# The opening of an eight-batch attention, gated MLP and expert-attention kernel: one written list of single steps for all engines

## The chip, the cores and the metric

The kernel runs on one core of a Trainium2 chip. The metric is the device time of one execution in microseconds. TensorE (PE in the profile) does the matrix products and transposes, VectorE (DVE) and ScalarE (ACT) work on their results, GpSimd (POOL) does small side work, and SyncE (SP) issues the transfers (DMAs); it has one queue, in which a transfer that waits holds up all behind it.

## What is computed

For each of eight batches: a packed attention (32 query rows `p` over the 576 rows of `k` and `v`, then `q` over the packed rows), an MLP whose second half is mixed over the tokens by `w_sg`, and a causal attention in each of four experts, of which two count per token.

```python
def sm_attn(qq, kk, vv): ...                       # softmax(qq kk^T / 8) vv
p_packed = sm_attn(p, k, v); x = sm_attn(q, p_packed, p_packed)   # [8, 576, 512] after the heads are joined
h = gelu(x @ w_in); u, v = h[..., :512], h[..., 512:]
v_n = (v - mean(v)) / sqrt(var(v) + 1e-6) * g_ln
gated = u * (einsum('ts,bsd->btd', w_sg, v_n) + b_sg)
x = x + gated @ w_out
# experts e: q, k, v = x @ wq[e], x @ wk[e], x @ wv[e]; causal softmax; ye = a @ v @ wo[e]; top 2 of 4 by x @ w_gate
```

## The kernel before

**Weights.** `moe_w_in` (two halves `f`: 0 makes u, 1 makes v; four tiles `j` each) and `moe_w_out` (four tiles `c`) come as 64-bit floats and are turned to 32 bits on VectorE and ScalarE: six VectorE instructions of 128x512 per tile (L150, L151, L160 to L163) and one on ScalarE (L155). `w_out` is then multiplied into the expert weights: `prep_w_out` transposes a tile, `fold` makes 4 products into PSUM (512, 256 and 4 columns), `fold_out` splits the result into a high and a low part. Products of split operands run in three passes (`PASSES`). `w_sg` is transposed by `prep_w_sg`, five tiles, and split too.

**Batch 0.** Steps named by letters in the table `STEP`: K (transpose k on TensorE), s (scores of p), n, a (transpose them), Q (transpose q), p (packed product), P (transpose it), m (scores of q, L448), x, r (their softmax on VectorE), h (split them). Then `w'` (`wp_mm`, L625: packed rows times `w_in`), the v products (`v_tiles`, L676), the token mixing (`vs_mm`, L744), the u products (`u_tile`, L726) and the gate. In `startup` these are written in one order, stage after stage.

**Batches 1 to 7.** k and q are not transposed on TensorE but in transfers: each of 16 heads (8 of k, 8 of q) is turned by a DMA transpose into a tile `kx` or `qx` (two buffers), which a second transfer writes to DRAM (`turned_k`, `turned_q`); `planes` loads them back (`kp`, `qp`), and GpSimd joins the two halves of each word (L416, 8 instructions for k and 8 for q). The turns are queued in the list `TURN`, one head per entry, each entry first writing out the head before:

```python
TURN.append([lambda a=last: a and keep(*a), lambda a=(name, src, h): turn(*a)])
```

`tick()` takes one entry. `back(0)`, after the gate, runs the last stage of batch 0 (`bdw`, the products `qk`, `vlog`) mixed with the packed attention of batch 1.

**What sets the order.** In `startup` only TensorE follows the written order (`manual_schedule(engines={ET.PE})`); the framework's scheduler orders the other engines and SP's queue. From `back(0)` on, TensorE and SP both follow the written order. PSUM has four working tiles (`pd`), and the SBUF tiles come from rings: the three buffers of tag "a" hold the raw `w_in` tiles, the two of "W" the expert weights of the folds and later `w_qk` and `w_vg`, the ten of "B" the softmax, the split v and `kp` and `qp`.

Of the kernel before, what the change touches and what calls it, by code (L numbers as in the profile page):

```python
# [7 lines left out]
F32 = mybir.dt.float32  # L8
# [18 lines left out]
def packed_attention_mlp_moe_kernel(  # L27
# [80 lines left out]
    nc.sync.dma_start(g_bc, dap(moe_g_ln, 0, [[0, P], [1, DM]]))  # L108
# [39 lines left out]
    def from_f64_top(raw, dst):  # L148
        hw, top = words(raw)[:, :, 1], dst.bitcast(I32)
        nc.vector.tensor_scalar(top, hw, 3, 0x3FFFFFF8, op0=OP.logical_shift_left, op1=OP.bitwise_and)  # L150
        nc.vector.scalar_tensor_tensor(top, hw, -0x40000000, top, op0=OP.bitwise_and, op1=OP.bitwise_or)  # L151

    def from_f64_abs(raw):
        hw = words(raw)[:, :, 1].bitcast(F32)
        nc.scalar.activation(hw, hw, AF.Abs)  # L155

    def from_f64_low(raw, dst, pw):
        lw, hw, top = words(raw)[:, :, 0], words(raw)[:, :, 1], dst.bitcast(I32)
        f = pw.bitcast(F32)
        nc.vector.tensor_scalar(pw, top, -0x800000, None, op0=OP.bitwise_and)  # L160
        nc.vector.scalar_tensor_tensor(f, lw.bitcast(U32), 2.0 ** -52, f, op0=OP.mult, op1=OP.mult)
        nc.vector.tensor_tensor(f, f, dst, op=OP.add)
        nc.vector.scalar_tensor_tensor(dst, hw.bitcast(F32), LEAST_F64, f, op0=OP.is_ge, op1=OP.mult)  # L163
# [26 lines left out]
    w_in = {}  # L190

    def w_in_steps(f):
        def top(j):
            w_in[f, j] = slot("D", w=512, name="w_in")
            from_f64_top(raw_in[f, j], w_in[f, j])

        def low(j):
            from_f64_low(raw_in[f, j], w_in[f, j], nat_slot(I32, "pw"))
            nc.sync.dma_start(kept[f"in{f}"][:, j, :], w_in[f, j])

        return top, lambda j: from_f64_abs(raw_in[f, j]), low
# [3 lines left out]
    def load_w_all():  # L205

        t = slot("W", name="fqk").rearrange("p (i e r d) -> p i e r d", i=2, e=E, r=4)
        g = slot("W", w=1040, name="fvg")
        v = g[:, :1024].rearrange("p (e r d) -> p e r d", e=E, r=4)
        for o, w in ((t[:, 0], moe2_wq), (t[:, 1], moe2_wk), (v, moe2_wv)):  # L210
            nc.sync.dma_start(o.rearrange("p e r d -> p e (r d)"), dap(w, 0, [[4 * D, P], [DM * D, E], [1, 4 * D]]))
        nc.sync.dma_start(g[:, 1024:], dap(moe2_w_gate, 0, [[4 * E, P], [1, 4 * E]]))
        for r in range(4):
            folded[r] = (t[:, :, :, r, :].rearrange("p i e d -> p (i e) d"), v[:, :, r, :],
                         g[:, 1024 + 4 * r:1028 + 4 * r])
# [13 lines left out]
    def prep_w_sg(c):  # L229
        n = TOK[c]  # L230
        st = wst[c]
        pw = pd("wsgT")
        pt, pl = pw[:, 0, :], pw[:, 1, :]
        for a in range(4):
            nc.tensor.transpose(pt[:, a * P:a * P + n], st[:n, a * P:(a + 1) * P], ident[:n, :n])
        nc.tensor.transpose(pl[:64, 0:n], st[:n, 512:576], ident[:n, :n])
        cols = slice(c * P, c * P + n)
        src = pt.rearrange("p (a t) -> p a t", a=4)[:, :, :n]
        act_copy(w_sg[0][:, 0:4, cols], src)
        lo_part(nc.vector, w_sg[1][:, 0:4, cols], src, w_sg[0][:, 0:4, cols])  # L240
        act_copy(w_sg[0][:64, 4, cols], pl[:64, :n])
        act_copy(w_sg[0][64:P, 4, cols], pl[:64, :n])
        lo_part(nc.vector, w_sg[1][:64, 4, cols], pl[:64, :n], w_sg[0][:64, 4, cols])
# [7 lines left out]
    def prep_bias():  # L251
        bb = bias["b"]
        bh = slot("t", F32R, name="bh")
        act_copy(bh[64:66, :], bb[64:66, :])
# [7 lines left out]
    woT = {}  # L262

    wos = {}

    def wo_top(c):
        wos[c] = slot("B", w=512, name="wo")
        from_f64_top(raw_out[c], wos[c])
        from_f64_abs(raw_out[c])

    def wo_low(c):
        from_f64_low(raw_out[c], wos[c], slot("t", I32, 512, name="pw"))

    def prep_w_out(c):

        wo = wos.pop(c)
        pt = pd("woT")[:, 0, :]
        for j in range(4):
            nc.tensor.transpose(pt[:, j * P:(j + 1) * P], wo.rearrange("p (a r) -> p r a", r=4)[:, j, :], ident)
        t = slot("B", w=512, name="woT")  # L280
        act_copy(t, pt)
        woT[c] = t

    fpt = {}

    def fold(c, parts=(0, 1)):

        if not W:
            weight_tiles("w_qk")
            weight_tiles("w_vg")  # L290
        if c not in fpt:
            fpt[c] = pd("fold")
        t, pt = woT[c], fpt[c]

        for i in parts:
            for k in ((0,), (1, 2))[i]:
                o = (pt[:, 0, :], pt[:, 1, :256], pt[:, 1, 256:260])[k]
                o = o if k == 2 else o.rearrange("p (e d) -> p e d", d=D)
                for j in range(4):
                    nc.tensor.matmul(o, t[:, j * P:(j + 1) * P], folded[j][k], start=j == 0, stop=j == 3,  # L300
                                     skip_group_check=True)

    def fold_out(c):
        pt = fpt.pop(c)
        for i, name in enumerate(("qk", "vg")):
            n = COLS[name]
            hi, lo = (x[:, c, :] for x in W["w_" + name])
            act_copy(hi, pt[:, i, :n])
            lo_part(nc.vector, lo, pt[:, i, :n], hi)
# [15 lines left out]
    def load_nat(name, src, b, j):  # L325
        if (b, name) == (0, "q"):
            t = slot("T", w=512, name=name)
        elif (b, name) == (0, "v"):
            if j % 2 == 0:
                NAT["v2"] = slot("A", name=name)  # L330
            t = NAT["v2"][:, (j % 2) * 512:(j % 2) * 512 + 512]
        elif (b, name) == (0, "k") and j >= 2:
            t = slot("D", w=512, name=name)
        else:
            t = nat_slot(F32, name)
        t = t.rearrange("p (h n) -> p h n", h=2)
        off = (b * H + 2 * j) * S * D
        NAT[name, b, j] = t
        if b:
            for h in range(2):  # L340
                nc.sync.dma_start(t[:, h].rearrange("p (c d) -> p c d", c=4),
                                  dap(src, off + h * S * D, [[D, P], [P * D, 4], [1, D]]))
            if j % 2 == 0:
                r = small.tile([P, 2, D], F32, tag="rem", name=name + "r", bufs=2)
                for h in range(2):
                    nc.sync.dma_start(r[:, h], dap(src, off + (512 + 32 * h) * D, [[S * D, 4], [D, 32], [1, D]]))
                NAT[name + "r", b, j // 2] = r.rearrange("p h d -> p (h d)")
            return
        nc.sync.dma_start(t, dap(src, off, [[4 * D, P], [S * D, 2], [1, 4 * D]]))
        if j % 2 == 0:  # L350
            if name == "v":
                r = small.tile([P, 2 * D], F32, tag="rem", name=name + "r", bufs=2)
            else:
                if "rem" not in NAT:
                    NAT["rem"] = sb.tile([P, 512], F32, tag="y", name="rem", bufs=NB["y"])
                i = 2 * "kq".index(name) + j // 2
                r = NAT["rem"][:, i * P:(i + 1) * P]
            nc.sync.dma_start(r, dap(src, off + 512 * D, [[S * D, 4], [2 * D, 32], [1, 2 * D]]))
            NAT[name + "r", b, j // 2] = r
# [6 lines left out]
    def tick(n=1):  # L366
        for _ in range(min(n, len(TURN))):
            for f in TURN.pop(0):
                f()

    def p1_steps(b):
# [47 lines left out]
        def transpose_in(name, Q):  # L419

            pt, pr = pd("natT"), pd("remT")
            for jj in range(2):
                nat = NAT.pop((name, b, 2 * Q + jj))
                for i in range(4):
                    nc.tensor.transpose(pt[:, jj, i * P:(i + 1) * P], nat[:, i // 2, (i % 2) * P:(i % 2) * P + P],
                                        ident)
            nc.tensor.transpose(pr[:, 0, :P], NAT.pop((name + "r", b, Q)), ident)
            for jj in range(2):
# [835 lines left out]
```

## Time and profile before

| what | value |
|---|---|
| median of 3 runs (lowest, highest) | 879.46 us (879.15, 879.69) |
| the profiled execution: its time, its span | 878.9 us, 877.0 us |
| PE busy, share of the span | 825.4 us, 94% |
| DVE busy | 583.3 us, 67% |
| ACT busy | 424.7 us, 48% |
| POOL busy | 188.4 us, 21% |
| mean granted TensorE clock | 0.981 |

The span runs from the first instruction to the last; what lies around it is 1.9 us. Of the page's 40 slices (21.9 us each) the first eight show PE at 4, 6, 8, 7, 9, 8, 8 and 9 tenths, and almost all later ones at 9: what TensorE doesn't do lies in the first fifth of the run. Busy time of PE is modelled, and it is no measure of its speed: a matmul at the lower clock counts as busier.

### The profile page before, as it was taken

Reading aid. Unit: us, or ns where it says so; the run is one execution under the profiler, and the core shown is the slowest. Engines: PE = TensorE matmul, PEld = TensorE weight load, DVE = VectorE, ACT = ScalarE, POOL = GpSimd, SP = SyncE. Lnnn points to the kernel's source line nnn. Section 1 sums busy time; section 2 is a strip of 40 time slices with the busy share of each in tenths; the row PEclk is TensorE's granted clock in tenths of the full one; section 3 lists DMA queues with packets and bytes.
Section 4 is the critical chain, followed back from the end, with each engine's and each line's share of the span. In section 5 each row is a group of like instructions: output and inputs, shape, how many; then the busy total and the mean of one; then the engine's idle time right before and its main releaser. Section 6 shows DMA issues by size and latency. Waiting matters only on the chain.

```text
span 877.0 us, 19165 instructions
## 1 busy us (share of the span) xinstructions
PE 825.4 (94%) x7517; PEld 697.9 (80%) x7517; DVE 583.3 (67%) x1387; ACT 424.7 (48%) x973; POOL 188.4 (21%) x272
## 2 busy tenths in 40 slices
PE   4687988999999999999999999999999999999987
PEld 2356877788888888888789888888789888888965
DVE  6766644876577674877477665867488566866265
ACT  2356332565436542655346552655346543745245
POOL 0002051312332151303322141404222141300000
PEclk9798889999999999999999999999999999999989
DMA  9886673537445563548245563549263660100001
GB/s 307 229 208 176 143 234 86 146 88 224 114 99 143 140 188 86 154 109 231 76 130 116 148 188 83 154 111 237 69 153 89 171 178 7 74 13 26 19 1 55
DMA packets 178725, 114.08 MB, mean 130 GB/s; under 512 B 118282, under 2 KB 166666, under 8 KB 175820
## 3 DMA queue, kind: packets, MB, share of 16 engines
q1 hardware_dynamic: 178636, 112.87, 48.0%
q8 instruction: 59, 0.97, 0.5%
q14 instruction: 30, 0.25, 0.1%
HBM read 68.26 MB, written 29.63 MB: 112 GB/s over the span
## 4 chain that ended last, share of the span: by engine, by line
PE 75%; DVE 5%; ACT 2%; issue 1%; POOL 0%; ACTq 0%; DVEq 0%; POOLq 0%
PE vs L744 10%; PE qk L789 10%; PE y L968 6%; PE vlog L832 6%; PE qk L801 5%; PE v L676 5%; PE o L999 5%; PE sc L885 4%; PE u L726 4%; PE aTp L939 4%; PE vlog L836 3%; PE sc L915 2%; PE wp L625 1%; PE aTp L953 1%; PE s L448 1%
## 5 line engine op out<-in xcount | busy, mean ns | idle before, releaser
L744 PE MATMUL vs<-w_sg,vnh 128*128 128x288 f32 x512 | 92.8, 304 | 0.7 <-DVE w_sg L85 0.7
L789 PE MATMUL qk<-gh,w_qk 128*128 128x288 f32 x512 | 92.7, 304 | 0.0
L789 PEld LDWEIGHTS qk<-gh,w_qk 128*128 128x128 f32 x512 | 76.2, 193 | 10.6 <-issue 7.1
L82 ACT ACTIVATE aT<-aTp 128x512 f32<-128x512 f32 (+4 forms) x160 | 60.9, 434 | 44.1 <-PE aTp L939 36.2
L744 PEld LDWEIGHTS vs<-w_sg,vnh 128*128 128x128 f32 x512 | 75.7, 191 | 5.3 <-issue 3.0
L416 POOL COPY kT<-kp 128x576 uint16<-128x576 uint16 x56 | 48.0, 921 | 147.4 <-DMA kp<-turned_k 98.1
L898 ACT ACTIVATE at<-sc,nm 128x256 f32<-128x256 f32 (+3 forms) x128 | 66.3, 524 | 26.7 <-DVE nm L889 21.1
L691 POOL TENSOR_TENSOR rstd<-rstd,mhalf 128x1 f32<-128x1 f32 x40 | 36.4, 917 | 152.8 <-DVE rstd L690 152.8
L968 PE MATMUL y<-aT,v 128*64 128x128 f32 (+2 forms) x960 | 61.6, 267 | 0.2 <-ACT aT L82 0.2
L902 DVE TENSOR_SCALAR at<-at,sm,gw 128x256 f32<-128x256 f32 (+3 forms) x128 | 60.1, 511 | 2.3
L832 PE MATMUL vlog<-w_vg,gh 128*128 128x260 f32 (+1 forms) x320 | 60.8, 287 | 0.0
L968 PEld LDWEIGHTS y<-aT,v 128*64 128x64 f32 (+1 forms) x960 | 48.4, 140 | 14.1 <-issue 7.6
L819 POOL CAST last_q<-qk 64x64 fp32r<-64x64 f32 x64 | 14.9, 233 | 196.6 <-ACT qk L809 103.1
L789 PE MATMUL qk<-gl,w_qk 128*128 128x288 f32 x256 | 55.6, 299 | 0.0
L744 PE MATMUL vs<-w_sg,vnl 128*128 128x288 f32 x256 | 55.3, 298 | 0.0
L889 DVE TENSOR_REDUCE nm<-sc 128x2 f32<-128x256 f32 (+3 forms) x64 | 52.6, 822 | 1.7
L999 PE MATMUL o<-w_o,y 128*128 128x512 f32 x192 | 52.5, 408 | 0.5 <-ACT y L978 0.5
L832 PEld LDWEIGHTS vlog<-w_vg,gh 128*128 128x128 f32 (+1 forms) x320 | 47.4, 178 | 3.5 <-issue 2.8
L885 PE MATMUL sc<-qk 64*128 64x256 f32 (+3 forms) x384 | 47.4, 352 | 0.0
L416 POOL COPY qT<-qp 128x576 uint16<-128x576 uint16 x56 | 44.6, 870 | 11.0 <-DMA qp<-turned_q 11.0
L939 PE MATMUL aTp<-ident,at 128*128 128x128 f32 x320 | 46.6, 277 | 0.0
L899 DVE TENSOR_SCALAR sm<-sm 128x2 f32<-128x2 f32 x64 | 16.4, 256 | 44.9 <-ACT at L898 44.5
(208 smaller groups left out, 1927.9 us busy)
## 6 DMA issues: line engine op xcount, KB each, us to landing
w_in<-kept_in SPq DMA_DIRECT2D x14, 1024.0 KB
w_qk<-kept_qk SPq DMA_DIRECT2D x8, 1024.0 KB
out_dram<-ot SPq DMA_DIRECT2D x32, 256.0 KB
turned_k<-kx SPq DMA_DIRECT2D x56, 144.0 KB
turned_q<-qx SPq DMA_DIRECT2D x56, 144.0 KB
kp<-turned_k SPq DMA_DIRECT2D x56, 144.0 KB
qp<-turned_q SPq DMA_DIRECT2D x56, 144.0 KB
v<-in_v_dram SPq DMA_DIRECT2D x56, 128.0 KB
```

Source lines behind the costliest of these rows:

```text
L82: nc.scalar.activation(o, i, AF.Copy, scale=scale)
L416: nc.gpsimd.tensor_copy(w[:, i], t[:, i].rearrange("p h n -> p (h n)"))
L744: nc.tensor.matmul(pt[:, h, :HALF], s["vn", c][x][:, cols], w_sg[y][:, c, hs(h)], start=(c, x, y) == (0, 0, 0), stop=False)
L789: nc.tensor.matmul(o[:, h, :], W["w_qk"][y][:, m, cols], s["g", m][x][:, hs(h)], start=first and (m, x, y) == (0, 0, 0), stop=not first an ...
L832: nc.tensor.matmul(pt[:n, ci, :260], s["g", m][x][:, c * P:c * P + n], W["w_vg"][y][:, m, :], start=(m, x, y) == (0, 0, 0), stop=False)
L885: nc.tensor.matmul(pt[:, e, :L], qs[x][r, j * P:L], ks[y][r, :L], start=i == 0, stop=i == 2)
L889: nc.vector.tensor_reduce(nm, pt[:, :, :L], axis=AX.X, op=OP.max, negate=True)
L898: nc.scalar.activation(ats[e][:, :L], pt[:, e, :L], AF.Exp, bias=nm[:, e:e + 1], accum_out=sm[:, e:e + 1])
L902: nc.vector.tensor_scalar(ats[e][:, :L], ats[e][:, :L], sm[:, e:e + 1], s["w"][:, j, 2 * pr + e:2 * pr + e + 1], op0=OP.mult, op1=OP.mult)
L939: nc.tensor.transpose(pt[:, e, c * P:c * P + P], ats[e][:, c * P:c * P + P], ident)
L968: nc.tensor.matmul(pt[64 * e:64 * e + 64, pr * w:pr * w + w], s["v2"][:m, c, col:col + D], s["aT", pr, e, j][c][:m, :], start=c == 0, stop ...
L999: nc.tensor.matmul(pt, ys[:, pr, x, :], W["w_o"][y][:, pr, :], start=i == 0, stop=i == 5)
```

## The change

The opening becomes one list of names (`ORDER`), each a single step for one engine, and all five engines follow it word for word (`manual_schedule` of PE, DVE, ACT, POOL and SP). The scheduler has no say in it any more.

- Steps are cut small: the 64-bit conversion is now upper, absolute, lower, join and guard (names ending in t, a, p, l, g).
- To GpSimd go: the join of each conversion (the addition L162 of before; 12 tiles), the subtraction of the maximum in the softmax of batch 0 (`Ss`), and the low parts of the softmax (`al`), of `w_sg` (`wl`) and of v (`vl`). Since GpSimd can't read PSUM, ScalarE makes a copy in SBUF first (`copied()` for `w_sg`; `vg` scaled in place for v).
- The v products and the token mixing go tile by tile (`v0`, `g0`, `vs3_0`, ...), two folds are put behind the v products, one of them behind the u products; the `w_sg` transposes are ahead of the v products.
- Batch 0's last stage no longer uses `middle` but a new order: the gated half of two qk products first, then `bdw`, then the packed halves; batch 1's scores between them.

```diff
+    def v_high_0(b, c):
+        ...
+        nc.scalar.activation(vg, vg, AF.Copy, scale=s.pop(("rstd", c)))
+        act_copy(hi, vg)
+    def v_low_0(b, c):
+        ...
+            lo_part(nc.gpsimd, lo, vg, hi)
...
+        def join():
+            nc.gpsimd.tensor_tensor(f, f, dst, op=OP.add)
...
+        def high():
+            pt = hold["t"]
+            act_copy(copied(), pt[:, 0, :].rearrange("p (a t) -> p a t", a=4)[:, :, :n])
+            act_copy(hi[:, 0:4, cols], copied())
+        def low():
+            lo_part(nc.gpsimd, lo[:, 0:4, cols], copied(), hi[:, 0:4, cols])
...
+        if b == 0:
+            weights(0, ("qk", "vg"))
+            tick(len(TURN))
+            do_all("K0")
+            qk_gated(b, 0, True)
+            do_all("s0 K1")
+            qk_gated(b, 2, True)
+            do_all("s1 a0")
+            bdw(b)
+            weights(b + 1, ("in1", "in0"))
+            nxt = attention(b)
+            do_all("a1")
+            qk_packed(b, 0, False)
+            qk_out(b, 0)
+            do_all("p0 Q0")
+            qk_packed(b, 2, False)
+            qk_out(b, 2)
+            keep_last_q(b, 0)
+            do_all("P0")
+            vlog(b, VT[2])
+            do_all("p1 r0 Q1")
+            vlog(b, VT[0])
+            do_all("P1 r1")
+            ahead(b + 2)
+            tick()
...
+    ORDER = """
+        Dwo1 Dk0 Dwo0 K0 Dp Kc0 wo1t Din11 pT wo1p wo0t wo0p pTc s0 in11t wo1a Dk1 sm0 K1 Din13 wo1l Dq0 wo0a in11p
...
+        wh3 wl2 wpl1 wTc2 in01t wo3p wo3a wl0 v0 in01p g0 v1 wv3 wo3l g1 in01l fh1 v2 g2 b0 b1 wl3 in01a v3 pw0 c0
...
     def startup():
-        st = lambda names: [STEP.pop((0, n))() for n in names.split()]
...
+        steps = first()
+        for n in ORDER.split():
+            steps[n]()
-    with tc.manual_schedule(engines={ET.PE}):
+    with tc.manual_schedule(engines={ET.PE, ET.DVE, ET.Activation, ET.Pool, ET.SP}):
         startup()
```

In `ORDER` a name that begins with D is a load, `kw` copies the expert weights to DRAM in 20 small transfers, `ki1` and `ki0` write the converted `w_in` there, `A` makes the turns of batch 1, each single `t` is a tick (there are nine), and `F` loads `kp` and the `v` of batch 1. Three places show what this does to the queues.

On SP's queue, where the heads of batch 1's k are turned (`kx` is the turned tile, `turned_k` its copy in DRAM), before has:

```order
L397 DMA_TRANSPOSE kx_1001<-in_k_dram 128x576
L397 DMA_TRANSPOSE kx_1005<-in_k_dram 128x576
L403 DMA turned_k10_1003<-kx_1001 128x576
L403 DMA turned_k10_1003<-kx_1005 128x576
L397 DMA_TRANSPOSE kx_1008<-in_k_dram 128x576
L397 DMA_TRANSPOSE kx_1012<-in_k_dram 128x576
```

and the change has, at the same place:

```order
L434 DMA_TRANSPOSE kx_747<-in_k_dram 128x576
L440 DMA turned_k10_749<-kx_747 128x576
L434 DMA_TRANSPOSE kx_792<-in_k_dram 128x576
L440 DMA turned_k10_749<-kx_792 128x576
L434 DMA_TRANSPOSE kx_806<-in_k_dram 128x576
L440 DMA turned_k12_808<-kx_806 128x576
```

The pairs have become single turns: the write of a head, which needs its turn landed, now stands ahead of the next head's turn.

Further down SP's queue, where the last heads of q are turned and the planes of k are loaded, before has:

```order
L397 DMA_TRANSPOSE qx_1050<-in_q_dram 128x576
L397 DMA_TRANSPOSE qx_1054<-in_q_dram 128x576
L403 DMA turned_q16_1052<-qx_1050 128x576
L403 DMA turned_q16_1052<-qx_1054 128x576
L409 DMA kp_1136<-turned_k10_1003 64x4x288 x2
L409 DMA kp_1139<-turned_k12_1010 64x4x288 x2
```

and the change has, after the eight heads of k, the first of q, four writes of `w_in` and the eight loads of `kp`:

```order
L354 DMA vr_1058<-in_v_dram 128x1x64 x2
L349 DMA v_1061<-in_v_dram 128x4x64 x2
L203 DMA kept_in0_110<-w_in_794 128x512
L203 DMA kept_in0_110<-w_in_659 128x512
L203 DMA kept_in0_110<-w_in_771 128x512
L203 DMA kept_in0_110<-w_in_895 128x512
L195 DMA w_qk_1138<-kept_qk_111 128x2048
L195 DMA w_vg_1140<-kept_vg_112 128x1040
L440 DMA turned_q10_993<-qx_991 128x576
L434 DMA_TRANSPOSE qx_1143<-in_q_dram 128x576
L440 DMA turned_q10_993<-qx_1143 128x576
```

Seven of the eight heads of q have moved behind the planes of k, the loads of `v`, the writes of `w_in` and the loads of `w_qk` and `w_vg`, which wait for the last fold on TensorE; `qp` follows the last head.

On TensorE, ahead of the v products of batch 0, before has (a second fold and then the v products follow):

```order
L625 MATMUL wp<-w_in,ppT 32x512 x8
L300 MATMUL fold<-fqk,woT 128x512 x4
L300 MATMUL fold<-fvg,woT 128x256 x4
L300 MATMUL fold<-fvg,woT 128x4 x4
L279 MATMUL woT<-ident,wo 128x128 x4
```

and the change has:

```order
L582 MATMUL wp<-w_in,ppT 32x512 x8
L247 MATMUL wsgT<-ident,wst 128x128 x4
L248 MATMUL wsgT<-ident,wst 64x128
L310 MATMUL fold<-fvg,wo 128x256 x4
L310 MATMUL fold<-fvg,wo 128x4 x4
L297 MATMUL woT<-ident,wo 128x128 x4
L638 MATMUL v<-wph,a2h 128x512 x2
```

Only two folds now stand ahead of the v products; the `w_sg` transposes, which followed them, are ahead.

## Rows read from the trace of the kernel before

**Rows 1.** Busy time by stretch: PE, PEld, DVE, ACT, POOL, then PEclk, DMA share, GB/s.
```profile
0.00:69.37 69.37, 44.60 (x336) 27.93 (x337) 45.45 (x112) 24.87 (x56) 1.66 (x12) 0.93 0.87 241
69.37:142.37 73.00, 59.14 (x495) 51.11 (x494) 43.37 (x94) 31.50 (x59) 17.56 (x25) 0.88 0.63 172
142.37:165.84 23.47, 23.04 (x221) 19.85 (x220) 17.61 (x46) 8.62 (x21) 6.62 (x10) 1.00 0.37 109
165.84:877.00 711.16, 698.62 (x6476) 599.03 (x6468) 476.84 (x1136) 359.71 (x837) 162.55 (x225) 1.00 0.44 116
...
36.77:42.40 5.63, 5.63 (x9) 2.44 (x10) 4.69 (x14) 0.67 (x1) 0.00 (x0) 0.63 0.83 227
```

**Rows 2.** Timeline of TensorE: start, duration, line, tiles, idle time before.
```profile
36.77 5.77 PE L300 MATMUL fold<-fqk,woT 128*128 128x512 f32 x8 [7.16 <-ACT woT L82]
...
63.30 3.70 PE L300 MATMUL fold<-fqk,woT 128*128 128x512 f32 x8 [2.04 <-ACT woT L82]
...
69.37 0.71 PE L676 MATMUL v<-wph,a2h 128*128 128x512 f32 x2
...
76.29 0.60 PE L235 MATMUL wsgT<-ident,wst 128*128 128x128 f32 x4
...
85.11 1.31 PE L744 MATMUL vs<-w_sg,vnh 128*128 128x288 f32 x4 [0.74 <-DVE w_sg L85]
...
112.96 1.09 PE L625 MATMUL bdq<-w_qk,ppT 64*32 64x512 f32 x16
...
142.37 1.25 PE L448 MATMUL s<-qT,ppT 64*32 64x288 f32 x32
...
165.84 0.73 PE L676 MATMUL v<-wph,a2h 128*128 128x512 f32 x2
```

**Rows 3.** Timeline of SP's queue in the opening.
```profile
36.65 0.65 SPq L223 DMA_DIRECT2D kept_qk<-in_moe_wq_dram  x1
...
44.61 0.63 SPq L223 DMA_DIRECT2D kept_vg<-in_moe_wv_dram  x1
...
59.57 2.53 SPq L397 DMA_TRANSPOSE kx<-in_k_dram  x2
...
102.93 0.80 SPq L403 DMA_DIRECT2D turned_q<-qx  x2
```

**Rows 4.** Timeline of SP's queue one batch later, where turns are single.
```profile
176.79 1.13 SPq L397 DMA_TRANSPOSE qx<-in_q_dram  x1
...
179.74 1.63 SPq L397 DMA_TRANSPOSE qx<-in_q_dram  x1
...
199.49 1.13 SPq L397 DMA_TRANSPOSE qx<-in_q_dram  x1
...
202.32 5.15 SPq L409 DMA_DIRECT2D kp<-turned_k  x8
```

**Rows 5.** Timeline of GpSimd: the join of batch 2's k, and a split.
```profile
170.92 2.99 POOL L85 TENSOR_TENSOR w_o<-wst,w_o 128x512 fp32r<-128x512 f32 x2 [6.57 <-ACT w_o L82]
...
206.12 3.10 POOL L416 COPY kT<-kp 128x576 uint16<-128x576 uint16 x4 [24.22 <-DMA kp<-turned_k]
```

**Rows 6.** Timeline of VectorE: a load that it waits for; one line beside GpSimd and alone.
```profile
30.64 0.43 DVE L150 TENSOR_SCALAR w_in<-raw_in 128x512 int32<-128x512 int32 x1 [1.96 <-DMA raw_in<-in_moe_w_in_dram]
...
172.75 1.71 DVE L692 SCALAR_TENSOR_TENSOR vg<-vg,mv,g_bc 128x512 f32<-128x512 f32 x1
...
175.84 0.74 DVE L692 SCALAR_TENSOR_TENSOR vg<-vg,mv,g_bc 128x512 f32<-128x512 f32 x1
```

**Rows 7.** Groups of VectorE and GpSimd instructions: count, busy us, mean ns.
```profile
L163 DVE SCALAR_TENSOR_TENSOR w_in<-raw_in,pw 128x512 f32<-128x512 f32 x8 | 5.2, 683 | 0.3 <-ACT raw_in L155 0.3
...
L160 DVE TENSOR_SCALAR pw<-w_in 128x512 int32<-128x512 int32 x8 | 3.2, 415 | 0.0
...
L535 DVE TENSOR_TENSOR bt<-bt,sm 128x576 f32<-128x576 f32 x4 | 3.0, 748 | 0.1
...
L525 POOL TENSOR_TENSOR bt<-bt,mx 128x576 f32<-128x576 f32 x14 | 16.3, 1161 | 130.4 <-DVE mx L523 125.1 <-DVE lg L841 5.3
```

More of the change, by code (lines that the diff above doesn't have):

```diff
@@ L284, in packed_attention_mlp_moe_kernel @@
[L284 to L309, printed above, removed]
+    def w_out_tile(c):
+        return slot("B" if c < 2 else "T", w=512, name="wo")
+    def fold_steps(c):
+        x = {}
+        def turn():
+            pt = x["t"] = pd("woT")[:, 0, :]
+            wo = w_out[c].rearrange("p (a r) -> p r a", r=4)
+            for j in range(4):
+                nc.tensor.transpose(pt[:, j * P:(j + 1) * P], wo[:, j, :], ident)
+        def turned():
+            x["w"] = w_out_tile(c)
+            act_copy(x["w"], x.pop("t"))
+        def mm(k):
+            if k == 0:
+                x["f"] = pd("fold")
+            pt = x["f"]
+            o = (pt[:, 0, :], pt[:, 1, :256], pt[:, 1, 256:260])[k]
+            o = o if k == 2 else o.rearrange("p (e d) -> p e d", d=D)
+            for j in range(4):
+                nc.tensor.matmul(o, x["w"][:, j * P:(j + 1) * P], folded[j, k], start=j == 0, stop=j == 3,
+                                 skip_group_check=True)
+        def parts():
+            if not W:
+                weight_tiles("w_qk")
+                weight_tiles("w_vg")
+            for i, name in enumerate(("qk", "vg")):
+                yield x["f"][:, i, :COLS[name]], W["w_" + name][0][:, c, :], W["w_" + name][1][:, c, :]
+        def high():
+            for p_, hi, _ in parts():
+                act_copy(hi, p_)
+        def low():
+            for p_, hi, lo in parts():
+                lo_part(nc.vector, lo, p_, hi)
+        return turn, turned, lambda: mm(0), lambda: (mm(1), mm(2)), high, low
@@ L369, in tick, with scores, pp_mm_, pp_out @@
                 f()
+    def scores(wT, mT):
+        pt = pd("s12")
+        for h in range(2):
+            a = 64 * h
+            for i in range(4):
+                nc.tensor.matmul(pt[32 * i:32 * i + 32, h, :HALF], wT[a:a + 64, 32 * i:32 * i + 32],
+                                 mT(i)[a:a + 64], start=True, stop=True, skip_group_check=True)
+        return pt[:, :, :HALF]
+    def pp_mm_(b, Q, a1t, a1r):
+        s = ST[b]
+        pt = s["ppp", Q] = pd("pp")[:, 0, :]
+        vr = NAT["vr", b, Q]
+        for c in range(4):
+            for i in range(4):
+                nc.tensor.matmul(pt[32 * i:32 * i + 32, :D], a1t[:, c * P + 32 * i:c * P + 32 * i + 32],
+                                 NAT["v", b, 2 * Q + i // 2][:, i % 2, c * D:(c + 1) * D], start=c == 0,
+                                 stop=False, skip_group_check=True)
+        for h in range(2):
+            for i in range(4):
+                g = slice(32 * i, 32 * i + 32)
+                nc.tensor.matmul(pt[g, :D], a1r[g, h, :], vr[g, h * D:(h + 1) * D], start=False, stop=h == 1,
+                                 skip_group_check=True)
+    def pp_out(b, Q):
+        s = ST[b]
+        t = s["pp2", Q] = small.tile([P, 2, D], F32, name="pp2", bufs=2)
+        pt, rs = s.pop(("ppp", Q)), s.pop(("rs", Q))
+        for i in range(2):
+            nc.vector.tensor_scalar(t[:, i, :], pt[:, :D], rs, None, op0=OP.mult)
+    def ppT_mm(b, Q):
+        s = ST[b]
+        s["ppTp", Q] = pd("ppT")[:, 0, :P]
+        nc.tensor.transpose(s["ppTp", Q], s.pop(("pp2", Q)).rearrange("p a d -> p (a d)"), ident)
+    def ppT_out(b, Q):
+        s = ST[b]
+        s["ppT", Q] = small.tile([P, P], F32, name="ppT", bufs=2)
+        nc.scalar.activation(s["ppT", Q], s.pop(("ppTp", Q)), AF.Copy)
     def p1_steps(b):
@@ L1095, in back, with do_all @@
             tick()
+        return nxt
+    def back(b, go):
+        def do_all(names):
+            for n in names.split():
+                if (b + 1, n) in STEP:
+                    STEP.pop((b + 1, n))()
+                elif n[0] in "STyo":
+                    go(n)
+        if b:
+            go("S1")
+            vs_tile(b, 0)
+            go("S3")
+            vs_tile(b, 1)
+            go("T1 y0 T2 S5")
+            vs_tile(b, 2)
+            go("T3 o0 S4 y1")
+            vs_tile(b, 3)
+        if b == 0:
[23 more added lines that the diff above has]
+            tick()
+        else:
+            nxt = middle(b, go, do_all)
         vlog(b, VT[1])
```

733 lines of the change are left out of this document (378 added, 355 removed).

## Prediction

> **What bounds it now.** I read first the busy times by stretch [rows 1]. From the first v product of batch 1 (165.84 us) to the end TensorE is busy for 698.6 of 711.2 us; its order there is the same in both kernels, so I let these 711 us stand. All that can be won lies ahead of 165.84, in three stretches. Until the first v product of batch 0 (69.37) TensorE works 44.6 us and stands still for 24.8; from there to the scores of batch 1's q (142.37) it stands still for 13.9, at a granted clock of 0.88; from there to 165.84 for 0.4 only. So 39 us of standing still are on offer, and a little clock: the fold at 36.77 comes after 7.16 us of waiting, gets a granted clock of 0.63 (between the levels 1.2 and 2.4 GHz), and takes 5.77 us for what takes 3.70 at 63.30 [rows 1, 2]. A long wait thus costs about 2.1 us more.
>
> Then the queue of SP, since batch 1 needs its k and q turned in transfers before TensorE can go on. Before, the copies of the weights (`kept`) go out 0.80 us apart (ten steps from 36.65 to 44.61), the first two heads are turned at 59.57, and all 16 are written by 103.7 [rows 3]: 44 us, which lie beside TensorE's work; at 142.37 TensorE waits for none of them. Where turns are single, as one batch later, a head costs more: from 176.79 to 199.49 seven steps, 3.24 us each [rows 4], since the write of a head waits until its turn has landed.
>
> **The change part by part.**
>
> *The way to batch 0's first v product.* The list loads k first and needs three of four w_out tiles and all of w_in's half 1 converted before `wpl`. VectorE decides this. Its instructions over 512 columns take 0.68 us with two inputs and 0.42 with one, those over 576 columns 0.75 [rows 7]; an upper or lower part is one of each, 1.1. It stops at the third w_out tile, `wo2`. Counted by the sizes in the code, before has 8.0 MB loaded when the third w_in tile arrives at 30.64 [rows 6]; the new queue has 8.4 MB up to `wo2`; 0.4 MB at 227 to 241 GB/s [rows 1] is 1.7 us, so 32.5. From there to the guard of `in10`: two parts of `wo2` 2.2, a maximum 0.75, two sums with their reciprocals 2.4, the bias about 1.6, three guards 2.0, `Sn0` 0.75, two narrow low parts 0.5: 10.2 us, so 42.7.
>
> *GpSimd beside VectorE.* A line of VectorE with both inputs in SBUF takes 0.74 us alone and 1.71 beside GpSimd's split [rows 6], whose two instructions took 2.99 us [rows 5]. A GpSimd instruction with two inputs over 576 columns takes 1.16 us [rows 7], one over 512 then 1.03: VectorE waited 0.97, for nearly a whole one. Met in the middle it would wait for half; I take 0.55 us lost on VectorE per us of GpSimd, between 0 (they never meet) and 1. Four of them lie in the last stretch: 4.3 us, a loss of 2.4, `in10` at 45.1. After it come `Sb0`, `Sn1`, `Sb1` (2.3), two low parts (0.5), `wo3` (1.1), `fl0` (1.1), `wpl1` (1.3): 51.3. **First v product at 51, before 69.4.**
>
> *From there to the last fold.* Before took 43.6 us from the first v product to the end of u (112.96). Out go the 8.8 us of w_sg transposes and their wait (76.29 to 85.11), in come two folds of 6.07 (63.30 to 69.37) with 0.7 each for their transposes [rows 2]: 48.3 us. TensorE reaches `w'` of half 0 after some 26 of them, at 77. VectorE has by then 23.4 us of statistics, scalings, conversions and low parts to do since 51.3, and GpSimd 12.4 us beside them (five joins, four low parts of v, three of w_sg), a loss of 6.8: 81.5. A new wait of 4.5 us, of which the old one at that place (in the 43.6) covers 1.5: **last fold done at 102**; 92.5 if GpSimd cost nothing.
>
> The extra copies on ScalarE (ten over 512 columns) lie beside these and cost nothing: ScalarE works 56 of the first 142 us [rows 1].
>
> *SP's queue.* This is where I expect the gain to go. Its last w_in load (`Din01`) reuses the buffer of `in10` and waits for that guard: 45.1. Behind it stand 20 copies at 0.70 (0.65, the bare issue, to 0.80 [rows 3]), 14.0, and `pn`, 1.4 with the load itself: the first turn at 60.5, no earlier than before. From there, in the queue's order:
>
> - eight single heads at 3.24: 25.9; the ninth turn, 1.2
> - eight `kp` 5.15 [rows 4], 0.64 each; the smaller ones I put at 0.57: four writes of w_in 2.3, six loads of v 3.3, four writes 2.3, `w_qk` and `w_vg` 1.0, the write of q's first head 0.4: 14.5
> - seven more heads: 22.7
> - the first two `qp` 1.3, landing 2.5 (the second `kp` goes out at 203.6, GpSimd begins at 206.12), four joins 3.1 [rows 4, 5]
>
> That is 71.2 us: q is there at **131.7**. By the other limit `w_qk` waits for the last fold (102), and the last 31.0 us of the sum come behind it: 133. I take 132.5. TensorE gets there at about 122 (some 20 us of products lie behind the last fold) and stands still some 10 us: the wait for data of batch 0 has become a wait for q of batch 1.
>
> *From the scores to batch 1's v products.* Before 23.5 us (142.37 to 165.84). The new list puts a `vlog` pair between the two halves of the scores, so the second transpose of the packed product (0.3) falls behind the first scores; and TensorE comes out of a long wait (2.1): 25.9.
>
> **Sum.** 132.5 + 25.9 = 158.4 against 165.84: 7.4 us less, 871.5 for the profiled execution's 878.9, and 872 on the median, which is 0.56 above it.
>
> **Rivals.** *SP's queue is not the limit.* Then TensorE goes on at 122 (or 112.5 with GpSimd free) and batch 1's v comes at 146 (136): 20 to 30 us less, 850 to 859. For it: turns in pairs took (103.7 - 59.57)/16 = 2.8 us a head with pauses for TensorE among them. Against it: the turns stand single in the new order, and the first step of [rows 4] took 2.95 us, with 24 transfers between k and q that before stood elsewhere. 7%.
>
> *GpSimd shuts VectorE out altogether.* If each us of GpSimd's two-input work stops VectorE for a whole us, `in10` comes 1.9 later, `w'` of half 0 another 5.6; the last fold ends at 109.5, q at 140.5, v at 166.4: 879.5 to 880, no change. The 1.71 for 0.74 in [rows 6] is such a case; against it speaks that the two engines meet anywhere in an instruction, and that two of the three stages of a conversion wait for each other anyway. 10%. The Trainium skill says this in SBUF — State Buffer, "Who interferes with whom": an instruction of VectorE with two SBUF inputs and a GpSimd one that reads SBUF exclude each other for the whole instruction. The row agrees for one instruction; what share of them meets is open. By that rule taken in full the sum would be that of this rival.
>
> *Slower: the turns of batch 1 crawl.* The weights' copies go in short packets, and the first turns are queued behind them; 15 steps of 3.9 us instead of 3.24 put q at 141.5 and batch 1's v behind 167; from there each 0.1 us a step costs 1.5. At 4.3 a step: 131.7 + 15.9 + 25.9 = 173.5, 886.6. For it: the seven steps' mean of 3.24 with a first of 2.95 means that some took longer; against it, the mean itself. 9%.
>
> **How the numbers follow.** The forecast, q's turns as the limit at 3 to 17 us of gain, has 74%. Its bounds: the guard of `in10` at 42, copies at 0.65, steps at 2.95 give q at 123.3, the fold limit with GpSimd free 123.5: 16.4 us less, 863; `in10` at 49, 0.80 and 3.5 give 141.5 and no gain. With the second rival inside, 8 in 10 lie between 863 and 880. A measurement here tells 0.2% (1.8 us) from no change: faster than 877.7 0.84 (forecast, first rival, and 3 of the second's 10 by its milder half), within 0.08, slower 0.08.
>
> **What would show it.** In the profile after: first v product of batch 0 near 51; a wait of some us ahead of `w'` half 0 put down to VectorE; SP's queue waiting in turn for each `kx` and `qx`, the first turn near 60; a wait of about 10 us of TensorE ahead of the scores of batch 1's q, released by GpSimd's join or by `qp`; a lower granted clock right behind it; and from batch 1's first v product the same 711 us. The prediction is wrong if TensorE doesn't wait there, if the first turn goes out far from 60, or if the first v product comes later than 60.

## The result and the profile after

The changed kernel takes 889.32 us (median of four, 888.07 to 893.63) against 879.58 for the kernel before on the same chip: a ratio of 1.0116, 95% interval 1.0086 to 1.0146. It is slower, where 872 us, a gain, was forecast. Its profiled execution is the slowest of the four (893.63 us, span 891.9), so the places below can lie up to 4 us later than in the median one.

First the windows of the kernel after, cut at batch 0's first v product, at the ends of TensorE's long stop, and at batch 1's first v product (columns as in [rows 1]):

```profile
0.00:54.44 54.44, 38.27 (x310) 24.58 (x310) 42.40 (x96) 29.76 (x69) 19.87 (x27) 0.97 0.88 255
54.44:127.34 72.90, 63.06 (x473) 51.24 (x472) 50.55 (x78) 32.49 (x55) 34.15 (x29) 0.98 0.60 145
127.34:149.94 22.60, 0.00 (x1) 0.03 (x1) 0.31 (x2) 0.38 (x1) 6.78 (x11) 0.62 0.70 203
149.94:178.70 28.76, 27.87 (x270) 22.98 (x270) 17.27 (x48) 8.22 (x21) 7.04 (x10) 0.89 0.39 99
178.70:891.90 713.20, 699.21 (x6476) 599.20 (x6468) 476.28 (x1136) 360.35 (x837) 162.89 (x225) 0.99 0.44 115
```

The last stretch answers to the 711.16 us of [rows 1]: 2.0 us more. Batch 1's first v product comes 12.9 us later (178.70 against 165.84); the two make the 14.9 us between the spans. Ahead of it the first two stretches work as the written list wants: batch 0's first v product comes 15 us earlier than in [rows 2]. TensorE is still idle for 16.2 us of the first and 9.8 of the second. Then TensorE, VectorE and ScalarE have next to nothing to do for 22.6 us; of GpSimd's 6.78, 6.1 are the joins of q.

TensorE's timeline names the step:

```profile
54.44 0.71 PE L638 MATMUL v<-wph,a2h 128*128 128x512 f32 x2
...
87.05 1.54 PE L582 MATMUL wp<-w_in,ppT 64*32 64x512 f32 x16
...
101.75 2.68 PE L310 MATMUL fold<-fvg,wo 128*128 128x256 f32 x16
...
122.34 0.65 PE L382 MATMUL pp<-v,a1t 128*32 128x64 f32 x32
...
149.94 2.22 PE L382 MATMUL pp<-v,a1t 128*32 128x64 f32 x32 [22.60 <-DMA v<-in_v_dram]
...
152.67 1.21 PE L372 MATMUL s<-qT,ppT 64*32 64x288 f32 x16
...
178.70 0.73 PE L638 MATMUL v<-wph,a2h 128*128 128x512 f32 x2
```

The stop stands at the second packed product (`pp`, `p1` in the code) and is put down to a load of v, not ahead of the scores of q (152.67), which follow without a wait. SP's queue shows why that load is late:

```profile
48.23 0.65 SPq L231 DMA_DIRECT2D kept_qk<-in_moe_wq_dram  x1
...
63.44 1.23 SPq L434 DMA_TRANSPOSE kx<-in_k_dram  x1
...
89.23 1.72 SPq L434 DMA_TRANSPOSE qx<-in_q_dram  x1
...
104.96 0.85 SPq L195 DMA_DIRECT2D w_vg<-kept_vg  x1
105.87 0.46 SPq L440 DMA_DIRECT2D turned_q<-qx  x1
106.38 2.03 SPq L434 DMA_TRANSPOSE qx<-in_q_dram  x1
115.23 0.34 SPq L440 DMA_DIRECT2D turned_q<-qx  x1
...
133.89 5.15 SPq L446 DMA_DIRECT2D qp<-turned_q  x8
139.14 1.02 SPq L195 DMA_DIRECT2D w_in<-kept_in  x2
140.25 1.37 SPq L349 DMA_DIRECT2D v<-in_v_dram  x2
141.67 2.55 SPq L354 DMA_DIRECT2D vr<-in_v_dram  x2
144.32 2.73 SPq L349 DMA_DIRECT2D v<-in_v_dram  x2
```

`p0` issues the loads of the second pair of v tiles, since the buffers `nat` come free behind the first product (done at 123.4). In SP's list they stand behind `tick(len(TURN))`, `qp` and `w_in`, and so go out at 140.25. The chain of waits, in which a row of a DMA runs from its issue to its landing, runs the same way: a turn that took 8.84 us to come through (four writes of `w_in`, 1 MB, and 1.5 MB of `w_qk` and `w_vg` went out in the 4 us ahead of it), six more turns, eight `qp`, two `w_in`, then v. The first six multiplications of the product start at 149.94, on the tile of v that has landed; the other 26 wait for the last one, until 151.1:

```profile
106.38 8.84 DMA qx<-in_q_dram
115.23 0.34 SPq L440
115.67 2.51 DMA qx<-in_q_dram
...
146.54 4.52 DMA v<-in_v_dram
151.10 1.06 PE pp L382 x26
```

### The profile page after: what moved, and what is told of

It is laid out like the page before. It is cut to its first block, busy times and chain, and to the rows that moved or that the text cites. A ratio compares the mean times of both kernels' runs of the same rounds, so it can differ in the third digit from the quotient of the medians.

```text
span 891.9 us, 19190 instructions
## 1 busy us (share of the span) xinstructions
PE 828.4 (93%) x7517; PEld 698.0 (78%) x7517; DVE 586.8 (66%) x1358; ACT 431.2 (48%) x983; POOL 230.7 (26%) x301
## 4 chain that ended last, share of the span: by engine, by line
PE 78%; DVE 9%; DMA 6%; SPq 2%; ACT 2%; issue 2%; ACTq 0%; DVEq 0%
PE vs L749 11%; PE qk L805 10%; PE vlog L848 6%; PE y L984 6%; PE qk L817 5%; PE v L638 5%; PE o L1015 5%; PE u L719 5%; PE sc L901 5%; PE aTp L955 4%; PE vlog L852 3%; DMA qx<-in_q_dram 3%; DMA v<-in_v_dram 2%; PE wp L582 2%; PE sc L931 2%
## 5 line engine op out<-in xcount | busy, mean ns | idle before, releaser
L453 POOL COPY kT<-kp 128x576 uint16<-128x576 uint16 x56 | 52.0, 996 | 164.1 <-DMA kp<-turned_k 140.5
L805 PE MATMUL qk<-gh,w_qk 128*128 128x288 f32 x512 | 90.9, 300 | 0.0
L918 DVE TENSOR_SCALAR at<-at,sm,gw 128x256 f32<-128x256 f32 (+3 forms) x128 | 62.3, 528 | 2.3
L848 PEld LDWEIGHTS vlog<-w_vg,gh 128*128 128x128 f32 (+1 forms) x320 | 48.3, 181 | 4.4 <-issue 3.3
L504 POOL TENSOR_TENSOR bt<-bt,mx 128x576 f32<-128x576 f32 x14 | 16.3, 1162 | 128.6 <-DVE mx L503 128.6
L817 PE MATMUL qk<-a2h,bdq 128*128 128x288 f32 x256 | 48.2, 308 | 1.3 <-DVE bdq L85 1.3
L854 ACT ACTIVATE v<-vlog 128x512 f32<-128x512 f32 (+1 forms) x24 | 12.4, 521 | 73.7 <-PE vlog L852 50.1
```

The source lines that it names most:

```text
L453: nc.gpsimd.tensor_copy(w[:, i], t[:, i].rearrange("p h n -> p (h n)"))
L805: nc.tensor.matmul(o[:, h, :], W["w_qk"][y][:, m, cols], s["g", m][x][:, hs(h)], start=first and (m, x, y) == (0, 0, 0), stop=not first an ...
L817: nc.tensor.matmul(o[:, h, :], s["bd", Q][y][:, cols], s["a2", Q][x][:, hs(h)], start=first and (Q, x, y) == (0, 0, 0), stop=not first and ...
L848: nc.tensor.matmul(pt[:n, ci, :260], s["g", m][x][:, c * P:c * P + n], W["w_vg"][y][:, m, :], start=(m, x, y) == (0, 0, 0), stop=False)
L918: nc.vector.tensor_scalar(ats[e][:, :L], ats[e][:, :L], sm[:, e:e + 1], s["w"][:, j, 2 * pr + e:2 * pr + e + 1], op0=OP.mult, op1=OP.mult)
```

## The experiments

Theory: SP's order holds the kernel, as in the prediction, but through v and not through q. Rival 1: the new order of the last stage costs by itself. Rival 2: GpSimd's share of the opening slows VectorE so that everything comes late. Each row gives the median, the ratio to the kernel before with its interval, and where batch 1's first v product stands in the profiled execution (before 165.84, after 178.70).

```
run                     us      ratio   95%                first v of batch 1
e1_v_first              881.96  1.0040  1.0022 to 1.0059   168.35
e2_w_in_later           884.99  1.0080  1.0064 to 1.0096   171.45
e3_turns_early          875.43  0.9977  0.9961 to 0.9993   164.53
e4_both                 868.90  0.9903  0.9879 to 0.9927   151.96
e5_old_last_stage       891.51  1.0144  1.0119 to 1.0169   177.52
e6_new_last_stage       878.55  0.9994  0.9975 to 1.0012   164.43
e7_both_vector          870.32  0.9911  0.9882 to 0.9941   156.41
e8_turn_first           893.43  1.0166  1.0141 to 1.0192   176.61
e9_before_late_turns    889.44  1.0119  1.0092 to 1.0147   177.31
e10_pairs               883.81  1.0061  1.0038 to 1.0084   169.38
e11_both_pairs          874.27  0.9939  0.9918 to 0.9960   159.31
e12_v_on_act            893.12  1.0160  1.0123 to 1.0197   178.93
```

**v ahead of the q turns.**

```diff
-        t = nat_slot(F32, name).rearrange("p (h n) -> p h n", h=2)
+        t = slot("T", w=512, name=name) if (b, name) == (1, "v") and j >= 2 else nat_slot(F32, name)
+        t = t.rearrange("p (h n) -> p h n", h=2)
...
-            for j in range(2):
+            for j in range(4 if b == 1 else 2):
                 load("v", v, j)
```

> The changed kernel, with one edit: batch 1's other two v tiles and their rest get buffers of their own (of the tag T) and are loaded with the first two, ahead of the q turns. Theory (SP's order): the 22.6 us that TensorE waits at the second packed product go, since v no longer stands behind seven q turns, eight qp and 2 MB of w_in. The six loads cost SP's queue 3.3 us more ahead of q, so the last turn is written at 137, the first two qp take 1.3 and land 2.5 later, GpSimd's joins take 3.1: TensorE now waits at the first scores of q instead, until about 144 (after: 152.7), batch 1's first v product at 170 (after: 178.7), 880 to 882 us in all. Rival 1 (the new order of the last stage costs by itself) and rival 2 (GpSimd slows VectorE): no change, 887 to 891.

Measured 881.96 us. In its timeline of TensorE the stop has moved to the scores of q, where the prediction had it, and GpSimd's join ends it:

```profile
141.16 1.17 PE L373 MATMUL s<-qT,ppT 64*32 64x288 f32 x4 [13.95 <-POOL qT L454]
...
168.35 0.73 PE L639 MATMUL v<-wph,a2h 128*128 128x512 f32 x2
```

So v was the later of two things that TensorE waits for, and q is the next. It comes 3 us earlier than expected: the last turn is written at 135.4 and not at 137, and the first scores start after half a join (139.55 to 142.58).

**w_in behind v.**

```diff
             bdw(b)
-            weights(b + 1, ("in1", "in0"))
...
             do_all("p0 Q0")
+            weights(b + 1, ("in1", "in0"))
```

> The changed kernel, with one edit: the two loads of w_in (1 MB each) are issued after the second pair of v tiles instead of ahead of it. Theory (SP's order): v is issued 1.1 us earlier and doesn't lie behind 2 MB, which at the 358 GB/s of that slice take 5.9 us; the wait at the second packed product ends at about 143.5 instead of 149.9, 882 to 884 us in all. Rivals 1 and 2: no change, 887 to 891.

884.99 us; the product has all its tiles at 143.91, where 143.5 was expected:

```profile
143.91 1.06 PE L382 MATMUL pp<-v,a1t 128*32 128x64 f32 x26 [0.91 <-DMA v<-in_v_dram]
```

The same 26 multiplications start at 151.10 in the profile after. Of the 7.2 us, 1.6 are a last q write that comes earlier in this execution (131.9 against 133.5), and 5.6 are the two loads of 1 MB that no longer stand ahead: v is issued sooner, and issuing its six loads takes 3.4 us instead of 6.8.

**The turns early**, the copies of the weights among them:

```diff
-        Dgbc wl1 Din00 Din02 in10g Din01 Sb0 Sn1 wh2 kw wv0 wp1 ah0 fh0 wv2 Sb1 wo3t w3 ah1 al0 fb1 wph1 al1 fl0 wT2
+        wl1 Din00 Din02 in10g Din01 kw A t k t k t k t k t k t k t k t k t k t k t t Sb0 Sn1 wh2 wv0 wp1 ah0 fh0 wv2
```

Here `kw` only makes the list of the 20 copies, and each `k` issues two of them. `A` and the single `t` of the later lines are gone, and two `t` stand right behind `F`.

> The changed kernel, with SP's queue reordered alone: the 20 copies of the weights are laid singly between the turns, two to a turn, and 12 turns stand ahead of the first kp instead of nine, two more ahead of the loads of w_qk. The second pair of v tiles stays where it is. Theory (SP's order): the first turn goes out at 50 instead of 63.4, the last turn is written at about 118 instead of 133.5, qp and w_in go out by 125 and v lands by 131: TensorE waits some 4 us at the second packed product and not at the scores; batch 1's first v product at 160, 870 to 873 us in all. Rival 1: the stop gets shorter but the time stays above 879. Rival 2: no change in the opening, since VectorE sets it, and TensorE waits for VectorE where it waited for data.

875.43 us, 2 more than expected: q is written by 120.9, but v still goes out behind `qp` and `w_in`, at 128.3, and takes TensorE 7.2 us at the second product, where 4 were expected:

```profile
135.68 0.84 PE L388 MATMUL pp<-v,a1t 128*32 128x64 f32 x4 [7.18 <-DMA v<-in_v_dram]
```

**Both together.**

> The edits of the first and third run of this set together: all four v tiles of batch 1 are loaded ahead of the last q turns, and the turns begin early. Theory (SP's order): no wait of more than 3 us is left at the second packed product, q's joins are done at about 131 and TensorE waits there 0 to 4 us; batch 1's first v product at 154 to 158, 866 to 871 us in all, faster than the kernel before. Rivals 1 and 2: not faster than 879.

868.90 us, faster than either kernel. SP's queue and TensorE of this run:

```profile
48.79 1.23 SPq L441 DMA_TRANSPOSE kx<-in_k_dram  x1
...
120.15 0.33 SPq L447 DMA_DIRECT2D turned_q<-qx  x1
```

```profile
126.59 0.65 PE L389 MATMUL pp<-v,a1t 128*32 128x64 f32 x32
...
127.53 0.82 PE L379 MATMUL s<-qT,ppT 64*32 64x288 f32 x16
...
151.96 0.73 PE L645 MATMUL v<-wph,a2h 128*128 128x512 f32 x2
```

Neither the product nor the scores wait. What the change had won in the opening now reaches the end: batch 1's first v product stands 13.9 us ahead of [rows 2] in this profiled execution, which is the fastest of its four (864.44); the median gains 0.97%.

**The last stage as before** (`back` calls `middle` for batch 0 too):

> The change without its last part: the written opening stays, the first batch's last stage is again in the order of the kernel before. Theory (SP's order): the second pair of v tiles still stands behind all q turns, qp and w_in, so TensorE stops at the second packed product until about 146 to 150, and what is left to do behind it is nearly the same: 886 to 892 us, as the changed kernel. Rival 1 (the new order of the last stage costs by itself): the time falls to 880 or below.

891.51 us: the opening alone is as slow as the whole change. TensorE waits twice:

```profile
111.54 1.96 PE L582 MATMUL bdq<-w_qk,ppT 64*32 64x512 f32 x16 [7.24 <-DMA w_qk<-kept_qk]
...
148.30 1.97 PE L382 MATMUL pp<-v,a1t 128*32 128x64 f32 x22 [9.54 <-DMA v<-in_v_dram]
```

The first wait is one that the new order hides: `w_qk` needs the buffer of the last fold, and the new stage has gated products to do meanwhile.

**The new last stage alone**, in the kernel before:

> The change's last part alone: the kernel before with the first batch's last stage in the new order (there all q turns are written by 104, ahead of it). Theory (SP's order): the second packed product stands only some 6 us behind the first, whose end lets the v loads go, and these stand behind qp and w_in: TensorE waits there 2 to 8 us, the rest is as in the kernel before; 878 to 885 us. Rival 1 (the stage's order costs by itself, 10 us): 887 or more.

878.55 us, no difference. With the turns written early its second product waits 0.3 us:

```profile
139.19 0.63 PE L490 MATMUL pp<-v,a1t 128*32 128x64 f32 x26 [0.32 <-DMA v<-in_v_dram]
```

Rival 1 falls by these two runs.

**GpSimd's new work back on VectorE**, in the kernel of the fourth run:

```diff
-            nc.gpsimd.tensor_tensor(f, f, dst, op=OP.add)
+            nc.vector.tensor_tensor(f, f, dst, op=OP.add)
```

and so the low parts of `w_sg` and of batch 0's v.

> The fourth run's kernel (v early, turns early) with what the change put on GpSimd back on VectorE: the joins of the conversions, the low parts of w_sg and of the first batch's v. GpSimd keeps the subtractions of the second softmax, its low parts and the powers. Up to the first batch's w' of half 0 these are 20 instructions of 0.68 us, 13.6 us more on VectorE; in the changed kernel VectorE's instructions of that stretch lost 15 us beside GpSimd, of which some 12 come back. Theory: no difference that can be told from the fourth run (866 to 872 us), first v product of batch 0 at 53 to 56. Rival 2 (GpSimd's share of the opening costs more than it takes off): 864 or less, first v product before 51.

870.32 us; its interval and that of the fourth run overlap nearly whole, and batch 0's first v product comes at 53.77 in one and 53.95 in the other (its profiled execution waits 5.0 us for `w_qk` at `bdq`, the fourth's does not, hence the two places in the table). The groups of VectorE from 54 to 92 us show what is exchanged, of the fourth run:

```profile
L667 DVE SCALAR_TENSOR_TENSOR vg<-vg,mv,g_bc 128x512 f32<-128x512 f32 x5 | 6.6, 1322 | 0.0
...
L655 DVE BATCH_NORM_STATS2 bnst<-vg 128x6 f32<-128x512 f32 x5 | 3.4, 680 | 0.0
```

and of this one:

```profile
L667 DVE SCALAR_TENSOR_TENSOR vg<-vg,mv,g_bc 128x512 f32<-128x512 f32 x5 | 3.7, 747 | 0.0
L655 DVE BATCH_NORM_STATS2 bnst<-vg 128x6 f32<-128x512 f32 x5 | 3.4, 688 | 0.7 <-ACT vg L650 0.7
```

The line with two inputs in SBUF costs 1322 ns beside a busy GpSimd and 747 alone; the statistics, with one input of the same size, cost the same in both. Not every line with one input does: the two `TENSOR_SCALAR` lines of the conversion take 645 and 669 ns in the fourth run and 417 and 421 here. Rival 2 falls: GpSimd takes from VectorE about what it takes off it.

**The turn ahead of the write**, a miss:

```diff
-TURN.append([lambda a=last: a and keep(*a), lambda a=(name, src, h): turn(*a)])
+TURN.append([lambda a=(name, src, h): turn(*a), lambda a=last: a and keep(*a)])
```

> The changed kernel, with one edit: the turn of a head is issued ahead of the write of the head before it, so that two turns are under way. Theory (SP's order): a head costs about 2.6 us of the queue instead of 3.1 to 3.2, the last q head is written 6 to 9 us earlier, and the v loads behind it too: the wait at the second packed product ends at 141 to 144, 881 to 884 us. If turns don't overlap, nothing changes (887 to 891).

893.43 us, nothing gained. There are two buffers `x`, so a turn now waits until the write issued just ahead of it has landed:

```profile
72.99 0.52 SPq L440 DMA_DIRECT2D turned_k<-kx  x1
74.95 1.14 SPq L434 DMA_TRANSPOSE kx<-in_k_dram  x1
```

A head costs 3.2 us again: the wait for the landing of a turn was exchanged for one for the landing of a write.

**The kernel before, with late turns**: in `startup` nine steps of the turns are issued in place of all, the others in `back`, behind the first v loads.

```diff
         ahead(1)
-        tick(len(TURN))
+        tick(9)
...
+        if b:
+            tick(len(TURN))
         if b + 1 < B:
             STEP.pop((b + 1, "f"))()
+        if b == 0:
+            tick(len(TURN))
```

> The kernel before, with nothing of the change, but with seven of batch 1's q turns issued where the changed kernel has them: behind the kp and the first v loads, ahead of w_in, qp and the second pair of v. Theory (SP's order): seven turns of 3.2 us push qp from 122 to about 139 and the second pair of v to 146, which lands behind 2 MB of w_in at some 150; TensorE waits 10 to 12 us at the second packed product, batch 1's first v product moves from 166 to 175 to 178: 887 to 892 us. If the changed opening or the last stage's order were the cause, this kernel would stay within 2 us of the kernel before.

889.44 us, the ratio of the change itself (1.0119 against 1.0116), with nothing changed but the place of the late turns:

```profile
131.60 0.33 SPq L403 DMA_DIRECT2D turned_q<-qx  x1
...
143.34 1.10 SPq L341 DMA_DIRECT2D v<-in_v_dram  x2
```

```profile
147.62 0.76 PE L490 MATMUL pp<-v,a1t 128*32 128x64 f32 x4 [9.43 <-DMA v<-in_v_dram]
...
177.31 0.72 PE L676 MATMUL v<-wph,a2h 128*128 128x512 f32 x2
```

Batch 1's first v product stands within 1.4 us of where the change has it (177.31 and 178.70), though TensorE reaches the second product at 138.2 here and at 127.3 there: what the new opening wins is spent in the wait.

**Turns in pairs** (two turns, then their two writes, for batch 1):

> The changed kernel, with one edit: batch 1's turns are issued in pairs (two turns, then their two writes) over the same two buffers, as the kernel before does from 59.6 to 103.7. Theory: what makes a single turn cost 3.1 to 3.2 us of the queue is that it waits for its own landing before the write; in pairs a head costs 2.5 to 2.8 (before: 5.05 for a pair of q from 84.2 to 89.3), the eight q heads are done 4 to 7 us earlier, the wait at the second packed product ends at 142 to 146, 882 to 886 us. If the write's landing is what counts (as the run with the turn ahead of the write hints), a pair costs 6.2 or more and nothing is gained: 888 to 893.

883.81 us, as expected, and the wait ends at 141.8:

```profile
141.79 2.26 PE L382 MATMUL pp<-v,a1t 128*32 128x64 f32 x32 [15.50 <-DMA v<-in_v_dram]
```

A pair of q goes out at 111.83 and the next at 116.34, 2.3 us a head; over the seven pairs that no other transfer divides it is 2.2 to 2.9.

**Pairs in the kernel of the fourth run**, a second miss:

> The fourth run's kernel (v early, turns early, the weights' copies between the turns) with batch 1's turns in pairs as in the tenth. Theory (SP's order): there TensorE waits for no transfer any more between batch 0's first v product and batch 1's, so a faster queue of turns gains nothing: 866 to 871 us, the same as the fourth run within its interval; batch 1's first v product at 150 to 155. If turns still were a limit, some 3 to 6 us less: 865 or below.

874.27 us where 866 to 871 were expected: none of its times lies below 871.79 and none of the fourth run's above 870.36, though the two intervals touch. With four copies of the weights between the turns and writes of a pair, a pair takes 7.6 to 9.7 us at first (57.28, 66.97, 75.40), the last q heads are written at 125.5, 5 us later than in the fourth run, and this is the row of waits that comes back:

```profile
PE s L379 <- POOL qT L460: 4.6, 2, 3.8
```

Its first v product of batch 0 also comes 3.2 us later (57.20 against 53.95), where no edit touches the way to it; that place moves by 3.6 us between these runs (53.59 to 57.20), and what moves it was not looked into. The two make up about the 7.4 us between the places in the table.

**v issued by ScalarE**, a third miss:

```diff
+        dma = nc.scalar if (b, name) == (1, "v") and j >= 2 else nc.sync
```

> The changed kernel, with one edit: the loads of batch 1's second pair of v tiles and their rest are issued by ScalarE instead of SP, so that they wait for the first product alone and not behind the q turns. They move the same bytes at nearly the place in time that the order of the program gives them. Theory (SP's order, not the transfers' own time): v is issued at about 123.5 and lands by 129, TensorE then waits at the first scores of q until about 140.7 (q's turns and qp begin where they do in the changed kernel and the joins of the first two end at 140.7), the first v product of batch 1 comes at 166 to 167: 877 to 881 us. If the stop were the bandwidth that qp, w_in and v share, v would still land late: 886 or more.

893.12 us. The four loads of v leave SP's queue but do not go out earlier (the two small rests do, at 96). ScalarE's rows and the chain:

```profile
140.57 5.56 ACTq L350 DMA_DIRECT2D v<-in_v_dram  x4
```

```profile
139.38 6.36 DMA w_in<-kept_in
...
145.75 6.16 DMA v<-in_v_dram
```

Four semaphore instructions stand at the line of these loads in ScalarE's queue, from 122.0 to 142.1, and the chain leads from the landing of the first `w_in` to the last of them. What the other three loads waited for, and why the program makes v wait for `w_in`, the trace does not show. So the run moved the issuing engine and kept the place behind `qp` and `w_in`: it tells nothing of bandwidth against order. The first two runs tell that the place in the order counts, since the same bytes in another order take the wait away (the first) or shorten it (the second).

## Why the prediction was wrong

**The step that failed** is in "SP's queue": "q is there at 131.7 ... TensorE gets there at about 122 ... and stands still some 10 us: the wait for data of batch 0 has become a wait for q of batch 1." The sum ended with what the scores need and left out the second pair of v, which TensorE needs one step earlier and SP issues later. The scores began at 152.67 and not at 132.5. Of the 20.2 us, 8.2 are q itself (its first join ends at 140.7 in the profile after), and 12.0 are v: two `w_in` and the v loads issued behind `qp`, the last of which lands at 151.1, and the rest of the product.

```profile
137.65 3.04 POOL L453 COPY qT<-qp 128x576 uint16<-128x576 uint16 x4 [14.26 <-DMA qp<-turned_q]
```

The trace of before held the warning in rows that were not read, of TensorE and of SP:

```profile
139.45 0.30 PE L490 MATMUL pp<-v,a1t 128*32 128x64 f32 x2 [1.00 <-DMA v<-in_v_dram]
```

```profile
133.84 1.86 SPq L341 DMA_DIRECT2D v<-in_v_dram  x2
```

There these loads go out when the first product lets them (133.8), and still come 1.5 us late at the second. A load that is just in time has no cover: whatever holds its queue past the moment at which it could go out is paid. The ninth run pays it in the kernel before: its seven late turns take 22 us of the queue (109.8 to 132.0), part of which it had stood waiting, and the v loads go out 9.5 us later than here (143.34).

**q's own 8.2 us** are terms of the right mechanism that were mis-sized. The first turn went out at 63.4, not 60.5: the guard of `in10` ended at 47.8, not 45.1 (the two bias lines on two partitions took 1.45 and 1.71 us beside GpSimd, 0.51 and 0.81 in the kernel before); the 20 copies then took 14.1, where 14.0 were put. The first eight heads took 25.8 (25.9), what stands between them and the second head of q 17.1 (15.7). The seven q heads behind `w_qk` and `w_vg` took 27.5 (22.7), 9.3 of it the first, for which the sum of 1.0 us for two issues had no landing. Together q came 9.0 later than the 131.7 of the sum, 8.2 later than the 132.5 that was taken. These terms alone would have used up the forecast gain of 7.4 us: in the first run, where v no longer holds TensorE, the kernel still takes 881.96 us and is slower than before (by its expectation, 3.3 us of that are the v loads that it puts ahead of q).

**What held.** Batch 0's first v product came at 54.4 (51), the last fold was done at 104.4 (102). VectorE lost beside GpSimd, from the six groups that lengthen between runs seven and four from 54 to 92, 9.7 us to 20.4 us more of GpSimd: 0.47 us per us, where 0.55 was taken. The agreement is in part luck, since 1.9 of the 9.7 us lie in lines with one input, which the sum left out. The Trainium skill, SBUF — State Buffer, "Who interferes with whom", has a VectorE instruction with two SBUF inputs contend with a GpSimd one that reads SBUF, and one with at most one input not, outside the two-port modes. The two pairs of groups shown with the seventh run agree; the two `TENSOR_SCALAR` lines, which lengthened with one input, would have to belong to its exception, and no run here shows in which mode they ran. Over the stretch the loss is about half of GpSimd's time. From the scores to batch 1's v product it was 26.0 us (25.9); from 149.94 to 156.50 the granted clock was 0.50 (the level of 1.2 GHz), behind it 1.00, so a lower clock came behind a long stop as forecast. TensorE arrived at its stop at 127.3 (122), 22.9 us behind the last fold where some 20 were put.

**What came out by luck.** From batch 0's first v product to the end of the last fold it took 50.0 us, where 51 were forecast, but not through the wait that was in the sum. None was left at `w'` of half 0, as TensorE came there at 87 and not at 77; on the way it stood still for 6.1 us in five waits, for ScalarE and GpSimd, which the sum did not have.

**The rivals.** The slower one ended on the right side by another mechanism: it let turns crawl at 3.9 to 4.3 us each, but they went at 3.0 to 3.2 on the mean, the first one behind `w_qk` aside, and the place behind them was late. The bounds of the range moved three terms of q's chain (the guard, the copies, the step of a turn) and had none for v, so 880 could not hold it. The lower bound has a slip of its own: the 92.5 for the last fold with GpSimd free does not follow from the terms shown, which give 95.7 (51.3 - 2.4 + 48.3 - 1.5), and so 866 instead of 863.

## What to carry to other kernels

When transfers change places in an in-order queue, list for each consumer behind them every load of that queue, and ask which one lands last and which landed just in time before: when one wait goes, the next one in the queue's order takes its place, not the one that one had in mind. Here an opening that brought TensorE 11 us earlier to the second product was worth nothing while the queue that feeds the next stage started no earlier; the same opening was worth 1% once the turns began at 49 us and v stood ahead of the last of them.

## What the runs showed that was not expected

A DMA transpose that was issued behind 2.5 MB of plain transfers took 8.84 us to come through, where the six behind it took 2.5 to 2.9. Turns and writes over two buffers cost about 3.2 us a head whichever of the two is issued first, and 2.2 to 2.9 in pairs. And giving loads to another engine's queue did not free them from the transfers ahead of them in program order: the last of the four went out when the first `w_in` had landed.
